# Attention and feed-forward on one core: the main loop in two 64-row tiles of the array, q and k work in fixed bursts

## The chip, the cores and the metric

The kernel runs on one core of one Trainium2 chip. A core has TensorE (PE in the profile; its weight loads are listed apart as PEld), VectorE (DVE), ScalarE (ACT), GpSimd (POOL) and SyncE (SP), which here only issues DMAs. The metric is the device time of one execution in microseconds (us).

## The reference

```
for each of 4 batches (N = 12480 rows, C = 128, 49 agents):
    a2k = softmax(scale * agents @ k.T)        # 49 x N
    agent_v = a2k @ v                          # 49 x 128
    q2a = softmax(scale * q @ agents.T)        # N x 49
    x = q2a @ agent_v                          # N x 128
h = x @ w_in                                   # 49920 x 2048
out = (h - tanh(h)) @ w_out                    # 49920 x 128
```

The softmaxes subtract the row maximum and divide by the sum plus 1e-9. All inputs are float32; w_in and w_out arrive as float64.

## The kernel before

Agent_v is never multiplied with q2a on its own: `project` forms agent_v @ w_in (49 x 2048) for each batch, and the first product of the loop is q2a with that. To keep float32 accuracy with the single-pass fp32r matmul, every operand is split into a high part, rounded to fp32r, and a low part, the rest.

**The loop.** Columns of the transposed problem are worked in 100 blocks of up to 500 (25 for each batch), and each block in 8 steps (`HP`), one for two of the 16 chunks of 128 hidden features: 800 steps in `fast`. Two blocks make a pair, 16 positions (`pos`). A step holds:

- `m1` (L534, L535): h, two PSUM banks of 128x500. The 98 rows are 49 of the high part of q2a and 49 of its low part (pT); the weights awh and awl hold the 49 rows of the projection twice. Four matmuls.
- `act`: ACT makes y = tanh (L544) and z = y squared (L546) for 1000 columns; DVE multiplies g = h * z (L549). (For the small h of these inputs h - tanh(h) is so approximated; a general path exists behind a run-time test and is not taken.)
- `high`: POOL rounds g to gh (L578). `low`, one step later: DVE makes gl = g - gh (L583).
- `m2`, a step later again: six matmuls of 128 rows into one accumulator (L596 gh with the low part of w_out, L597 gh with the high part, L598 gl with the high part). The first block and one step of every second block use one float32 product instead (L594), without gh and gl.
- `finish`: ACT copies the accumulator out (L754), and one store is issued for two blocks.

**Beside it.** For each pair of blocks `q_softmax` works on q: scores on PE (L490), row maximum on DVE (L498), copy out of PSUM on ACT (L499), subtraction on POOL (L501), exp, sum and division, rounding and low part (L511, L513); `q_transpose` makes pT (L521, L526). For the next batch `phase1` makes the k scores (L278, with their copy and maximum), later exp, transposes (L329) and the product with v (L339), one group of eight 128-row tiles at a time.

**What sets the order.** The jobs are generators; a step advances every live job once between `m1` and `act`. A scheduler orders the instructions of each engine from that; only for the first block is the order on DVE and ACT, and up to there on PE, tied to the program (`issue_order`). PSUM's eight banks are three two-bank buffers for h and two single banks ("misc") for accumulators, q, k and transposes. Matmuls on all 128 rows and columns have one tile shape; the k bursts L278 and L339 use two column tiles of 64.

Of the kernel before, what the change touches and what calls it, by code (L numbers as in the profile page):

```python
# [12 lines left out]
F32 = mybir.dt.float32  # L13
# [11 lines left out]
A = 49  # L25
A2 = 2 * A
EARLY = 11
HALF = 64
FF = 2048
# [6 lines left out]
NG = -(-NT // GT)  # L36
TAIL = N - KT * 128
# [17 lines left out]
KV = 3  # L55
# [4 lines left out]
LAG2 = 1  # L60
NB = dict(y=2, z=2, g=4, gh=3, gl=2)
# [4 lines left out]
QS = 3  # L66
T0 = 13
T1 = 2
KS = (4, 10, 15)
VS = (5, 10, 13)  # L70
# [26 lines left out]
class Build:  # L97
    def __init__(self, ctx, tc, aps):
# [6 lines left out]
        self.ph = ctx.enter_context(self.pool("ph", 3, space=PSUM))  # L105
        self.pmisc = ctx.enter_context(self.pool("pmisc", 2, space=PSUM))
# [6 lines left out]

    def misc(self):
        return self.pmisc.tile([128, 512], F32, tag="misc", name="misc")

    def constants(self):
# [13 lines left out]
        self.ones = c.tile([128, 128], F32, tag="ones", name="ones")  # L131
        nc.vector.memset(self.ones, 1.0)
# [7 lines left out]
        self.avs = c.tile([128, B, A2], F32, tag="avs", name="avs")  # L140
# [54 lines left out]
    def phase1(self, b):  # L195
# [36 lines left out]
        def scores(g):  # L232
            yield
            yield
            if g == 0:
                st["s"] = self.keep.tile([128, NG * 512], F32, tag="s", name="s", bufs=1)
                if b == 0:
                    st["mxp"] = self.work.tile([128, A, 2 * NG], F32, tag="mxp", name="mxp", bufs=1)
                else:
                    st["mxp"] = self.small.tile([128, NG], F32, tag="mxk", name="mxk")  # L240
                st["acc"] = self.small.tile([128, C + 1], F32, tag="acc", name="acc")
            n = tiles(g)
            kt = ahead("k", load_k, g, 1 if b == 0 else kb - 1)
            if b and g >= NG - vb:
                ahead("v", load_v, 0, g - NG + vb + 1)
            if b == 0:
                ps = self.ph.tile([128, 2, 512], F32, tag="h", name="h")
# [24 lines left out]
                return  # L272
            ps = self.misc()
            w = n // 2 * 128
            for c in range(n // 2):
                for r in range(2):
                    to = ps[HALF * r : HALF * (r + 1), c * 128 : (c + 1) * 128]
                    nc.tensor.matmul(to, self.agz[:, b, :], kt[:, n // 2 * r + c, :], start=True, stop=True)  # L278
            yield
            nc.scalar.copy(st["s"][:, g * 512 : g * 512 + w], ps[:, :w])  # L280
            nc.vector.tensor_reduce(st["mxp"][:, g : g + 1], ps[:, :w], axis=AX.X, op=ALU.max)
# [34 lines left out]
        def av(g):  # L316
            vt = ahead("v", load_v, g, vb - 1) if b else None
            n = tiles(g)
            if b:
                w = n // 2 * 128  # L320
                e = st["s"][:, g * 512 : g * 512 + w]
                first = self.count()
                nc.scalar.activation(e, e, AF.Exp, bias=st["mb"], scale=SCALE)
                self.hold(first, self.act_at, (ET.Activation,))
                yield
                ps = self.misc()
                for c in range(n // 2):
                    sl = slice(c * 128, (c + 1) * 128)
                    nc.tensor.transpose(ps[:, sl], e[:, sl], self.ident)  # L329
                yield  # L330
                et = self.small.tile([128, 512], F32, tag="ke", name="ke")
                nc.scalar.copy(et[:, :w], ps[:, :w])
                yield
                ps = self.misc()
                for c in range(n // 2):
                    for r in range(2):
                        t = n // 2 * r + c
                        k = rows(g, t)
                        nc.tensor.matmul(  # L339
# [294 lines left out]
    def fast(self):  # L634
# [86 lines left out]
        for tag in ("y", "z", "g"):  # L721
            self.wtile(tag, NB[tag])
# [180 lines left out]
```

## Time and profile before

| | |
|---|---|
| median of 3 runs | 2153.54 us (2152.6 to 2153.64) |
| span of the profiled execution, first to last instruction | 2150.6 us |
| PE busy at a granted clock of | 0.998 of full speed |
| start of the first block's first matmul | 54.4 us |

The page gives the profiled execution its span and no time of its own; the median of the runs is 2.9 us above it. In the lines below a group is a line of the kernel, an engine, an operation, the tile written and the tiles read, the shapes, and the count; behind the first bar stand the busy time and the mean duration in ns, behind the second the idle time of the engine ahead of the group and what ended it. A line of the timeline has the start and the duration in us ahead of the same names. "Busy" of PE counts a matmul until its modelled end, so two that follow each other closely overlap.

### The profile page before, as it was taken

The page shows a single profiled execution, that of the slowest core. Times are in us where ns is not written, and L with a number is a line of the kernel's source. Part 1 is how long each engine was busy: PE and PEld are TensorE (multiplying, and loading weights), DVE is VectorE, ACT ScalarE, POOL GpSimd, SP SyncE. Part 2 cuts the span into 40 slices and gives each one's busy share as a digit, 9 for nine tenths or more (in the row PEclk, how much of TensorE's full clock was granted, in tenths as well). Part 3 has the DMA queues.
Part 4 walks back from the last instruction along what each step waited for, and adds up shares of the span by engine and source line. Part 5 has one row for each costly group of instructions (what it writes and reads, how often), then busy time and mean ns, then how long its engine had stood idle before and what let it go on. Part 6 is the DMA issues. An engine that isn't in the chain of part 4 may idle for free.

```text
span 2150.6 us, 30293 instructions
## 1 busy us (share of the span) xinstructions
PE 2126.8 (99%) x10859; PEld 1713.6 (80%) x10859; DVE 1998.3 (93%) x2031; ACT 1828.1 (85%) x2136; POOL 1313.8 (61%) x858
## 2 busy tenths in 40 slices
PE   8999999999999999999999999999999999999998
PEld 7587878877877887888787778878878888888886
DVE  7999998889999998889999999988999999999998
ACT  3888888888888888888898888888889889899896
POOL 0365566556665565556675557655566767777666
PEclk9999999999999999999999999999999999999999
DMA  9321112110111111111002110111000000000000
GB/s 350 96 67 60 52 34 73 51 49 29 39 49 59 60 50 49 59 61 49 20 20 68 59 42 28 51 59 41 28 31 20 29 30 20 29 29 20 29 10 21
DMA packets 65325, 108.69 MB, mean 51 GB/s; under 512 B 3984, under 2 KB 44176, under 8 KB 65168
## 3 DMA queue, kind: packets, MB, share of 16 engines
q1 hardware_dynamic: 65168, 106.68, 15.1%
q8 instruction: 89, 1.46, 0.3%
q14 instruction: 68, 0.56, 0.1%
HBM read 81.10 MB, written 25.56 MB: 50 GB/s over the span
## 4 chain that ended last, share of the span: by engine, by line
PE 95%; DVE 2%; POOL 1%; issue 1%; ACT 0%; DMA 0%; POOLq 0%; SPq 0%; DVEq 0%
PE h L534 17%; PE h L535 16%; PE misc L598 16%; PE misc L596 15%; PE misc L597 15%; PE misc L594 4%; PE misc L490 4%; PE misc L339 2%; PE misc L278 2%; PE misc L521 1%; PE h L249 1%; POOL gh L578 1%; DVE g L549 1%; PE misc L329 1%; DVE gl L583 1%
## 5 line engine op out<-in xcount | busy, mean ns | idle before, releaser
L578 POOL TENSOR_SCALAR gh<-g 128x1000 fp32r<-128x1000 f32 (+1 forms) x743 | 1172.7, 1579 | 702.9 <-DVE g L549 357.9
L583 DVE TENSOR_TENSOR gl<-g,gh 128x1000 fp32r<-128x1000 f32 (+1 forms) x743 | 952.8, 1284 | 99.9 <-PE misc L598 58.9
L549 DVE TENSOR_TENSOR g<-h,z 128x1000 f32<-128x1000 f32 (+1 forms) x800 | 946.1, 1187 | 24.6 <-ACT z L546 20.6
L544 ACT ACTIVATE y<-h 128x1000 f32<-128x1000 f32 (+1 forms) x800 | 799.0, 1002 | 191.6 <-PE h L535 187.6
L546 ACT ACTIVATE z<-y 128x1000 f32<-128x1000 f32 (+1 forms) x800 | 828.8, 1040 | 21.2 <-DVE g L549 4.2
L534 PE MATMUL h<-pT,awh 98*128 98x500 f32 (+1 forms) x1600 | 662.1, 414 | 0.1
L535 PE MATMUL h<-pT,awl 98*128 98x500 f32 (+1 forms) x1600 | 623.1, 389 | 0.0
L598 PE MATMUL misc<-gl,wo_h 128*128 128x500 f32 (+1 forms) x1486 | 589.5, 397 | 3.7 <-DVE gl L583 3.7
L596 PE MATMUL misc<-gh,wo_l 128*128 128x500 f32 (+1 forms) x1486 | 579.0, 390 | 2.8 <-POOL gh L578 2.8
L597 PE MATMUL misc<-gh,wo_h 128*128 128x500 f32 (+1 forms) x1486 | 578.1, 389 | 0.0
L534 PEld LDWEIGHTS h<-pT,awh 98*128 98x128 f32 x1600 | 301.2, 188 | 77.4 <-issue 14.0
L535 PEld LDWEIGHTS h<-pT,awl 98*128 98x128 f32 x1600 | 303.0, 189 | 67.7 <-issue 14.7
L598 PEld LDWEIGHTS misc<-gl,wo_h 128*128 128x128 f32 x1486 | 279.1, 188 | 70.0 <-DVE gl L583 10.5
L596 PEld LDWEIGHTS misc<-gh,wo_l 128*128 128x128 f32 x1486 | 280.8, 189 | 62.6 <-POOL gh L578 7.8
L597 PEld LDWEIGHTS misc<-gh,wo_h 128*128 128x128 f32 x1486 | 279.7, 188 | 54.5
L501 POOL TENSOR_TENSOR qe<-qe,qm 126x392 f32<-126x392 f32 x50 | 69.7, 1395 | 65.3 <-ACT qe L499 65.3
L513 POOL TENSOR_TENSOR pp<-qe,pp 126x392 fp32r<-126x392 f32 x50 | 67.8, 1357 | 58.4 <-ACT pp L511 56.6
L490 PEld LDWEIGHTS misc<-ag,qt 128*126 128x126 f32 x800 | 95.9, 190 | 3.9
L490 PE MATMUL misc<-ag,qt 128*126 128x49 f32 x800 | 93.4, 269 | 0.0
L594 PE MATMUL misc<-g,wo_f 128*128 128x500 f32 (+1 forms) x196 | 89.9, 581 | 0.0
L754 ACT ACTIVATE o<-misc 128x500 f32<-128x500 f32 (+1 forms) x100 | 58.2, 582 | 21.7 <-PE misc L598 11.7
L526 ACT CAST pT<-misc 98x500 fp32r<-98x500 f32 (+1 forms) x100 | 56.7, 568 | 7.4 <-PE misc L521 6.5
(111 smaller groups left out, 840.5 us busy)
## 6 DMA issues: line engine op xcount, KB each, us to landing
kt<-kT SPq DMA_DIRECT2D x48, 512.0 KB, 3.7
qt<-qT SPq DMA_DIRECT2D x46, 500.0 KB, 3.4
outT<-o SPq DMA_DIRECT2D x46, 500.0 KB, 2.6
v<-v SPq DMA_DIRECT2D x36, 512.0 KB, 4.1
vt<-v SPq DMA_DIRECT2D x12, 512.0 KB, 7.1
raw<-w_in SPq DMA_DIRECT2D x4, 512.0 KB, 9.0
v<-w_out SPq DMA_DIRECT2D x4, 512.0 KB, 8.9
qt<-qT SPq DMA_DIRECT2D x4, 490.0 KB, 3.4
```

Source lines behind the costliest of these rows:

```text
L490: nc.tensor.matmul(ps[:TT, t * A : (t + 1) * A], qt[:, at : at + TT], self.ag[:, b, :], start=True, stop=True)
L534: nc.tensor.matmul(h[:, c, :w], aw[0][:A2, sl], pT[:A2, :w], start=True, stop=False)
L535: nc.tensor.matmul(h[:, c, :w], aw[1][:A2, sl], pT[:A2, :w], start=False, stop=True)
L544: nc.scalar.activation(self.pair(y), h, AF.Tanh, scale=TSC)
L546: nc.scalar.activation(z, y, AF.Square)
L549: nc.vector.tensor_tensor(self.pair(g), h, self.pair(z), ALU.mult)
L578: self.nc.gpsimd.tensor_scalar(gh, g, 1.0, 0.0, ALU.mult, ALU.add)
L583: self.nc.vector.tensor_tensor(gl, g, gh.bitcast(F32), ALU.subtract)
L594: nc.tensor.matmul(acc[:, :w], wf[:, c * C : (c + 1) * C], gh[:, x], start=first, stop=last)
L596: nc.tensor.matmul(acc[:, :w], self.wo_l[:, f, :], gh[:, x], start=first, stop=False)
L597: nc.tensor.matmul(acc[:, :w], self.wo_h[:, f, :], gh[:, x], start=False, stop=False)
L598: nc.tensor.matmul(acc[:, :w], self.wo_h[:, f, :], gl[:, x], start=False, stop=last)
```

## The change

- **First product.** `m1` has three terms for each chunk, all of 49 rows: awh with the low part, awl with the high part, awh with the high part. The matmuls of the first chunk use rows 0 to 48, those of the second rows 64 to 112, each with its own PSUM bank, in turn. For this pT holds the high part in rows 0 to 48 and the low part in rows 64 to 112, and two DMAs make pb, the same with the halves swapped. awh and awl hold their 49 rows at 0 and at 64.
- **Second product.** `m2` cuts each matmul into rows 0 to 63 and 64 to 127 with an accumulator each (two banks). ACT copies both (1000 columns), POOL adds them, and each block has its own store. It follows four steps behind `m1`, not two.
- **PSUM** is one pool of four two-bank buffers for everything; within one step all jobs may share a buffer.
- **q and k work.** k is worked two groups at a time, in 7 score and 7 product jobs for a batch; a job starts at positions 4 and 9, q at position 2, the transposes at 2 and 12. Jobs start inside the step, ahead of `act`. At the end the order of PE, DVE and ACT is tied to the program for the whole loop.
- The square is made in place (no z); gh has 4 buffers, gl and y 3.

```diff
-LAG2 = 1
-NB = dict(y=2, z=2, g=4, gh=3, gl=2)
+LAG2 = 3
+NB = dict(y=3, g=4, gh=4, gl=3)
...
-KS = (4, 10, 15)
-VS = (5, 10, 13)
+T0 = 12
+KS = (4, 9)
...
-        self.ph = ctx.enter_context(self.pool("ph", 3, space=PSUM))
-        self.pmisc = ctx.enter_context(self.pool("pmisc", 2, space=PSUM))
+        self.ph = ctx.enter_context(self.pool("ph", 4, space=PSUM))
+        self.share(False)
...
     def misc(self):
-        return self.pmisc.tile([128, 512], F32, tag="misc", name="misc")
+        if self.spare is not None:
+            ps, self.spare = self.spare, None
+            return ps
+        t = self.banks("misc")
+        if self.sharing:
+            self.spare = t[:, 1, :]
+        return t[:, 0, :]
...
         yield
-        pT = self.keep.tile([128, BLK], F32R, tag="pT", name="pT", bufs=3)
-        nc.scalar.copy(pT[:A2, :w], ps[:A2, :w])
-        res.append(pT)
+        pT = self.keep.tile([128, BLK], F32R, tag="pT", name="pT", bufs=2)
+        nc.scalar.copy(pT[:PW, :w], ps[:PW, :w])
+        pb = self.keep.tile([128, BLK], F32R, tag="pb", name="pb", bufs=2)
+        nc.sync.dma_start(pb[HALF:PW, :w].bitcast(F32), pT[:A, :w].bitcast(F32))
+        nc.sync.dma_start(pb[:A, :w].bitcast(F32), pT[HALF:PW, :w].bitcast(F32))
+        res.append((pT, pb))
...
-        for c in range(2):
-            sl = slice((2 * i + c) * 128, (2 * i + c + 1) * 128)
-            nc.tensor.matmul(h[:, c, :w], aw[0][:A2, sl], pT[:A2, :w], start=True, stop=False)
-            nc.tensor.matmul(h[:, c, :w], aw[1][:A2, sl], pT[:A2, :w], start=False, stop=True)
+        h = self.banks("h")
+        high, low = pT, pT[::-1]
+        for n, (weights, p) in enumerate(((aw[0], low), (aw[1], high), (aw[0], high))):
+            for c, r in enumerate((slice(0, A), slice(HALF, PW))):
+                sl = slice((2 * i + c) * 128, (2 * i + c + 1) * 128)
+                nc.tensor.matmul(h[:, c, :w], weights[r, sl], p[c][r, :w], start=n == 0, stop=n == 2)
...
+            terms = (low, gh), (high, gh), (high, gl)
+        for k, (weights, g) in enumerate(terms):
+            for c in range(2):
+                f = 2 * i + c
+                for r in range(2):
+                    rows = slice(HALF * r, HALF * (r + 1))
+                    nc.tensor.matmul(
+                        acc[:, r, :w],
+                        weights(f, c)[rows],
+                        g[rows, c * w : (c + 1) * w],
...
-            nc.scalar.activation(o[:, at : at + w], acc[n][:, :w], AF.Copy, scale=GSC)
...
+            nc.scalar.activation(o[:, :, :w], acc[n][:, :, :w], AF.Copy, scale=GSC)
+            nc.gpsimd.tensor_tensor(o[:, 0, :w], o[:, 0, :w], o[:, 1, :w], ALU.add)
+            nc.sync.dma_start(self.outT[:, column(n) : column(n) + w], o[:, 0, :w])
...
+            self.share(True)
+            if p + 1 < npair:
+                if pos == QL and p:
+                    qt[p + 1] = self.q_load(q_src(p + 1))
+                if pos == T0:
+                    live.append(t_job(2 * p + 2))
+                if pos == T1 and p:
+                    q = q_job(p + 1)
+                    next(q)
+                    live.append(q)
+            if pos == T1 and p:
+                live.append(t_job(2 * p + 1))
+            if pos in KS and kq and n:
+                live.append(kq.pop(0))
...
         finish(done.pop(0))
+        self.issue_order(ET.PE, early)
+        self.issue_order(ET.DVE, at)
+        self.issue_order(ET.Activation, at)
```

In the changed kernel the lines are L576 for the first product, L638 for the second, L585 and L586 for tanh and square, L588 for g, L617 for gh, L622 for gl, L525 for the q scores, L533, L534 and L536 for their maximum, copy and subtraction, L558 and L563 for the transposes and pT, L792 and L793 for the copy and the add at the end of a block. Names carry buffer numbers here; a row in brackets names the engines whose semaphores it waits for.

DVE before, around the maximum of a q job in the third batch (g_11333 belongs to one step, g_11366 to the next):

```order
L549 TENSOR_TENSOR g_11333<-h_11319,z_11331 128x1000 [waits Activation_49]
L498 TENSOR_REDUCE qm_11324<-misc_11289 126x8 [waits PE_49]
L583 TENSOR_TENSOR gl_11337<-g_11307,gh_11309 128x1000 [waits PE_49,Pool_49]
L549 TENSOR_TENSOR g_11366<-h_11345,z_11364 128x1000 [waits Activation_49]
L583 TENSOR_TENSOR gl_11370<-g_11333,gh_11335 128x1000 [waits PE_49,Pool_49]
```

DVE of the changed kernel, the same job (g_14127 belongs to position 2, g_14165 to position 3):

```order
L588 TENSOR_TENSOR g_14127<-h_14104,y_14124 128x1000 [waits PE_49,Activation_49]
L622 TENSOR_TENSOR gl_14131<-g_14086,gh_14088 128x1000 [waits PE_49,Pool_49]
L533 TENSOR_REDUCE qm_14152<-misc_14111 126x8
L588 TENSOR_TENSOR g_14165<-h_14145,y_14162 128x1000 [waits PE_49,Activation_49]
L622 TENSOR_TENSOR gl_14169<-g_14127,gh_14129 128x1000 [waits PE_49,Pool_49]
```

The maximum stood between a g and a gl and now stands directly ahead of a g.

ACT before, at the copy of the same job's scores:

```order
L544 ACTIVATE y_11362<-h_11345 128x1000 [waits PE_49]
L546 ACTIVATE z_11364<-y_11362 128x1000 [waits DVE_49,Activation_49]
L499 COPY qe_11325<-misc_11289 126x392 [waits DVE_49]
L544 ACTIVATE y_11386<-h_11378 128x1000 [waits PE_49]
L546 ACTIVATE z_11388<-y_11386 128x1000 [waits Activation_49]
L503 ACTIVATE qe_11325<-qe_11325 126x392 [waits Pool_49]
```

ACT of the changed kernel, at the same place:

```order
L586 ACTIVATE y_14124<-y_14124 128x1000 [waits Activation_49]
L534 COPY qe_14153<-misc_14111 126x392 [waits DVE_49,PE_49]
L563 CAST pT_14157<-misc_14111 113x500 [waits DMAHW5_49,DMAHW4_49]
L585 ACTIVATE y_14162<-h_14145 128x1000 [waits PE_49]
L586 ACTIVATE y_14162<-y_14162 128x1000 [waits Activation_49]
L792 ACTIVATE o_14190<-acc_13944 128x1000 [waits DMAHW7_49,PE_49,Pool_49]
```

The copy waits for DVE's maximum in both. Before, the tanh and square for the g behind the maximum (y_11362, z_11364) stand ahead of the copy; in the changed kernel (y_14162) they stand behind it and behind the copy of pT.

PE of the changed kernel at the same position: first product, q burst with transposes, second product.

```order
L576 MATMUL h_14104<-pb_13966,awh_11386 128x500 [waits DVE_49]
L576 MATMUL h_14104<-pT_13964,awh_11386 128x500
L576 MATMUL h_14104<-pT_13964,awl_11387 128x500
L576 MATMUL h_14104<-pb_13966,awl_11387 128x500
L525 MATMUL misc_14111<-ag_67,qt_14053 126x49 [waits DVE_49]
L558 MATMUL misc_14111<-identr_75,pp0_95 113x126 x4
L638 MATMUL acc_13944<-gh_14002,wo_l_86 128x500 [waits Pool_49]
L638 MATMUL acc_13944<-gh_14002,wo_h_85 128x500 x4
```

The q scores now stand between the two products of one step and wait for a g of DVE, since their PSUM buffer is one that h uses too.

270 lines of the change are left out of this document (132 added, 138 removed).

## The prediction

> **What bounds the kernel now.** I read the busy shares and the chain of work first, then the busy times by stretch, then the groups of instructions, then the timeline where one duration had to be understood.
>
> ```profile
> span 2150.6 us, 30293 instructions
> PE 2126.8 (99%) x10859; PEld 1713.6 (80%) x10859; DVE 1998.3 (93%) x2031; ACT 1828.1 (85%) x2136; POOL 1313.8 (61%) x858
> PE 95%; DVE 2%; POOL 1%; issue 1%; ACT 0%; DMA 0%; POOLq 0%; SPq 0%; DVEq 0%
> core 0: us, PE busy (x) PEld busy (x) DVE busy (x) ACT busy (x) POOL busy (x), PEclk, DMA share, GB/s
> 130.00:2120.00 1990.00, 1987.07 (x10004) 1604.68 (x10003) 1865.43 (x1846) 1727.18 (x1990) 1262.53 (x814) 1.00 0.13 41
> 1669.40:2100.20 430.80, 430.80 (x2004) 352.43 (x2003) 415.17 (x396) 383.58 (x429) 303.14 (x188) 1.00 0.07 25
> 657.00:1631.00 974.00, 972.55 (x5010) 782.10 (x5007) 903.78 (x907) 838.79 (x978) 594.06 (x390) 1.00 0.14 45
> ```
>
> The reader is to see two things. PE is busy 1987 of the 1990 us of the loop and makes 95% of the chain: it sets the pace. But DVE is close behind it, 1865 of 1990. In the last batch (1669 to 2100), where no k work runs, it is at 96%; in the middle stretch, with k work, at 93%. So whatever is taken off PE, DVE's idle time in the loop, 1990 - 1865.4 = **124.6 us**, is the most that can come out before DVE is the bound. A later loss on DVE counts in full.
>
> **PE, part by part.** One pair of chunks (a "step", 800 in all) costs PE four matmuls for the first product and six for the second.
>
> ```profile
> L534 PE MATMUL h<-pT,awh 98*128 98x500 f32 (+1 forms) x1600 | 662.1, 414 | 0.1
> L535 PE MATMUL h<-pT,awl 98*128 98x500 f32 (+1 forms) x1600 | 623.1, 389 | 0.0
> 1000.75 0.38 PE L534 MATMUL h<-pT,awh 98*128 98x500 f32 x1
> 1000.97 0.39 PE L535 MATMUL h<-pT,awl 98*128 98x500 f32 x1
> 1001.20 0.39 PE L534 MATMUL h<-pT,awh 98*128 98x500 f32 x1
> 1001.20 0.19 PEld L535 LDWEIGHTS h<-pT,awl 98*128 98x128 f32 x1
> ```
>
> From start to start a 500-column matmul takes 0.227 us (1000.97 - 1000.75 is 0.22, the next 0.23); the 0.39 is latency. The first product becomes six matmuls of 49 rows in three pairs, one of each pair in rows 0 to 48 and one in rows 64 to 112. If a pair costs what one full matmul costs, a step saves one 0.227 us: 800 x 0.227 = 182 us of PE. The second product has twelve matmuls of 64 rows in six pairs, so it stays at six slots. The trace of before has no pair of row tiles; the nearest are its column tiles.
>
> ```profile
> L278 PE MATMUL misc<-kt,ag 128*64 128x128 f32 x588 | 41.6, 280 | 0.0
> 227.97 0.39 PE L535 MATMUL h<-pT,awl 98*128 98x500 f32 x1
> 228.29 1.09 PE L278 MATMUL misc<-kt,ag 128*64 128x128 f32 x16
> 229.32 0.50 PE L598 MATMUL misc<-gl,wo_h 128*128 128x500 f32 x1
> 229.65 0.39 PE L596 MATMUL misc<-gh,wo_l 128*128 128x500 f32 x1
> ```
>
> Sixteen of them, 0.28 us each, are through in 1.09 us: two halves of the array work at once, loads too. I take the pair at one slot; the bounds are one slot and two. The same rows price a change of tile shape: L535 to L278 takes 0.32 instead of 0.23, L598 to L596 0.33 instead of 0.23, and something is lost at the burst's own end; I take 0.3 us for going out of a shape and back. Before, only the k bursts leave the common shape, 81 times in the loop by the order of the program; after, every q, transpose, k and projection burst does, 168 times: 87 x 0.3 = 26 us more. PE so falls by some 156 us, to about 1831 of the old 1990. It is no longer the bound, and the time does not follow it.
>
> **DVE.** Its work per step is untouched: one L549 (now L588) and one L583 (now L622). What is moved is the q softmax. In the changed order DVE runs the row maximum of the q scores (L533), and directly behind it the product g of that step (L588). ACT stands q's copy out of PSUM (L534) and a copy of pT (L563) ahead of that step's tanh and square, and the copy waits for DVE's maximum. So g waits for a chain that starts with the instruction before it: maximum, copy, copy, tanh, square, g. Nothing else stands between on DVE. In the order of before the tanh and square of the next g stand ahead of the copy, and a gl (L583) follows the maximum, so the chain is covered.
>
> ```profile
> L499 ACT COPY qe<-misc 126x392 f32<-126x392 f32 x50 | 23.9, 479 | 25.4 <-DVE qm L498 25.4
> L526 ACT CAST pT<-misc 98x500 fp32r<-98x500 f32 (+1 forms) x100 | 56.7, 568 | 7.4 <-PE misc L521 6.5
> L544 ACT ACTIVATE y<-h 128x1000 f32<-128x1000 f32 (+1 forms) x800 | 799.0, 1002 | 191.6 <-PE h L535 187.6
> L546 ACT ACTIVATE z<-y 128x1000 f32<-128x1000 f32 (+1 forms) x800 | 828.8, 1040 | 21.2 <-DVE g L549 4.2
> ```
>
> The first row shows that the wait for the maximum is real in before too (25.4 us). The gap is 0.48 + 0.57 + 1.00 + 1.04 = 3.09 us, less a tenth where ACT's instructions overlap: 3.0 us for each of 48 q jobs in the loop, **144 us** of idle DVE (bounds: 0 if DVE had to idle there anyway, 149 without the overlap).
>
> **The new add on POOL.** ACT now copies both accumulators (1000 columns instead of 500), and POOL adds them, 128x500 from two inputs, 100 times. Before has four such instructions in the loop, L190.
>
> ```profile
> L190 POOL TENSOR_TENSOR wo_l<-awh,wo_h x4: 1278/1290/1293, 81.3 to 96.7; 128x512 fp32r<-128x512 f32 x4
> L583 DVE TENSOR_TENSOR gl<-g,gh x743: 1141/1191/2272, 84.2 to 2142.1; 128x1000 fp32r<-128x1000 f32 x179, 128x960 fp32r<-128x960 f32 x7
> 93.43 1.29 POOL L190 TENSOR_TENSOR wo_l<-awh,wo_h 128x512 fp32r<-128x512 f32 x1
> 93.59 2.18 DVE L583 TENSOR_TENSOR gl<-g,gh 128x1000 fp32r<-128x1000 f32 x1
> 1707.47 1.19 DVE L583 TENSOR_TENSOR gl<-g,gh 128x1000 fp32r<-128x1000 f32 x1
> 1708.57 1.19 DVE L549 TENSOR_TENSOR g<-h,z 128x1000 f32<-128x1000 f32 x1
> 1709.68 1.19 DVE L583 TENSOR_TENSOR gl<-g,gh 128x1000 fp32r<-128x1000 f32 x1
> L578 POOL TENSOR_SCALAR gh<-g 128x1000 fp32r<-128x1000 f32 (+1 forms) x743 | 1172.7, 1579 | 702.9 <-DVE g L549 357.9
> ```
>
> A gl that meets L190 takes 2.18 us instead of 1.19: it stands still for 1.0 us. Bounds for an add: nothing, where it falls beside a g, and 1.0. I take three of four adds to be met: 100 x 0.78 = **78 us**, near the upper end because a DVE without idle time leaves few openings: g and gl alternate every 1.11 us, and POOL's own gh needs the openings already. All gl together lose 743 x (mean 1.284 - median 1.191) = 69 us in before, mostly around gh and the two q operations of POOL. One of those now falls into the 3.0 us gap, where no gl runs: I take off 20 us of the 69 (bounds 0 and 35).
>
> The Trainium skill, page "SBUF — State Buffer", section "Who interferes with whom", says that a VectorE instruction with two SBUF inputs and a GpSimd one that reads SBUF exclude each other for a whole instruction. The 2.18 us row agrees; by the rule at its worst every add costs its whole 1.29 us, 129 us instead of 78, and the time would be some 51 us longer.
>
> **Edits at nothing.** The square in place and the deeper rings (gh 4, gl 3, second product four steps behind the first instead of two) leave the instructions as they are. The two transfers per block that build the swapped copy pb are 98 KB:
>
> ```profile
> ag<-agT SPq DMA_DIRECT2D x1, 98.0 KB, 2.3
> kt<-kT SPq DMA_DIRECT2D x48, 512.0 KB, 3.7
> ```
>
> They are issued one step after the transposes, three steps (8 us) or more before the block starts, and land in about 2.3 us; SP's queue ahead of them holds k, v, q loads and the stores, which wait for work of the same or an earlier step. If that cover is gone, each block start loses up to 1 us, 100 us. The k loads now come two together, five steps (13 us) before their use, against 3.7 us; their burst of two groups replaces two bursts. ACT's doubled copy, 100 x 0.42 = 42 us (L544's 1.00 less L754's 0.58), lies in ACT's idle time of 263 us in the loop; at the end it and the add make the tail 1.7 us longer.
>
> ```profile
> L754 ACT ACTIVATE o<-misc 128x500 f32<-128x500 f32 (+1 forms) x100 | 58.2, 582 | 21.7 <-PE misc L598 11.7
> ```
>
> **The sum**, on the profiled 2150.6 us: - 124.6 (DVE's idle time, freed with PE) + 144 (gap) + 78 (adds) - 20 (q operation in the gap) + 2 (tail) = 2230.0. The median of the runs is 2153.54, 2.9 above the span; I add it: **2233 us**, 3.7% slower.
>
> **Rivals.**
> *The saving comes through (ends faster).* DVE and POOL alternate without meeting, at the pace of 1706 to 1712, where every gl takes 1.19: then the adds cost nothing and the old 69 us go too. 2150.6 - 124.6 + 144 - 69 + 2 + 2.9 = 2106. It decides below 48 us of such waits in all (2150.6 - 124.6 + 144 + 2 = 2172 without the 69, against 2150.6: the waits must fall by 21 from 69, adds included). For it: that stretch exists. Against it: 100 more POOL instructions. Chance 0.22; no change, where the waits come out just there, 0.06.
> *More stalls.* The four two-bank PSUM buffers hold h, accumulator and bursts. In the step of a burst h has two buffers, the burst waits for a g of two steps before, and the second product is queued behind it. With 0.5 to 1 us of idle DVE for each of 168 bursts: +84 to +168, 2317 to 2401. Before has the same shortage only in part, so I give it 0.12.
> *Row tiles take turns.* If two 49-row halves did not work at once, a step would hold 18 slots instead of 10: 2150.6 + 800 x 8 x 0.227 + 2.9 = 3606 us. PE becomes the bound over DVE once a pair costs about 0.26 us instead of 0.227 ((2230 - 1995) / 7200 pairs = 0.033; 1995 is 2150.6 less PE's 156). For it: no row of before shows two row tiles at work. Against: the column tiles. Chance 0.06.
> The Trainium skill, page "TensorE: Matmul & The Clock Gate", section "LDWEIGHTS (loading the stationary operand)", says that a load's time follows its columns and not its rows, which speaks against cutting by rows: 18 loads of 128 columns per step instead of 10. The 98- and 128-row loads of before both take 0.19, so the trace agrees; one after the other they would hold 18 x 0.19 = 3.4 us of a step, and PE would take some 900 us more.
>
> **How the numbers follow.** Forecast 0.54 for 2165 to 2310 us, the rivals as given. The range, 2105 to 2310, takes in the price of an add from 0 to 1.3 and the waits of gl from none to more than now; it leaves out most of the last two rivals and a little below. About 0.2% is what a measurement of this kernel can tell from no change. Faster 0.22, within 0.2% 0.06, slower 0.72 (0.54 + 0.12 + 0.06).
>
> **What would show it.** Right: DVE is the largest share of the chain, PE's busy share falls below 97%, g (L588) idles about 140 us on ACT's square, once per pair of blocks, ACT's q copy waits for the maximum, and the mean gl rises above 1.30 us beside the add. Wrong: PE still fills the loop (a pair costs more than one slot), the idle before g is small, or gl's mean falls to 1.19.

## The result, and the profile after

| | before | changed |
|---|---|---|
| median of the runs, us | 2153.59 (4 runs, 2152.6 to 2154.4) | 2374.47 (4 runs, 2372.66 to 2375.54) |
| ratio | 1 | 1.1022, 95% interval 1.1007 to 1.1038 |
| span of the profiled execution, us | 2150.6 | 2373.5 |

10.2% slower, where 3.7% was forecast and 2310 us was the upper end of the range. The page of the changed kernel, then its waits and the busy times of its loop:

```profile
PE 2108.6 (89%) x17145; PEld 1692.9 (71%) x17145; DVE 2023.3 (85%) x2003; ACT 1863.6 (79%) x2082; POOL 1553.5 (65%) x961
PE 35%; DVE 33%; ACT 16%; issue 13%; DMA 2%; POOL 0%; SPq 0%; DVEq 0%; ACTq 0%; POOLq 0%
L588 DVE TENSOR_TENSOR g<-h,y 128x1000 f32<-128x1000 f32 (+1 forms) x800 | 953.2, 1192 | 292.6 <-ACT y L586 284.2
L622 DVE TENSOR_TENSOR gl<-g,gh 128x1000 fp32r<-128x1000 f32 (+1 forms) x743 | 963.9, 1297 | 16.9 <-PE acc L638 14.9
L793 POOL TENSOR_TENSOR o<-o 128x500 f32<-128x500 f32 (+1 forms) x100 | 126.0, 1260 | 92.1 <-ACT o L792 92.1
L534 ACT COPY qe<-misc 126x392 f32<-126x392 f32 x50 | 24.4, 487 | 194.2 <-DVE qm L533 145.4
```

```profile
DVE g L588 <- ACT y L586: 284.2, 211, 3.1
PEld h L576 <- DVE g L588: 132.9, 136, 2.5
PE h L576 <- DMA pb<-pT: 7.3, 9, 1.1
```

```profile
130.00:2340.00 2210.00, 1972.31 (x16055) 1584.55 (x16053) 1894.76 (x1827) 1766.12 (x1943) 1494.65 (x911) 0.97 0.15 46
```

(A wait: total us, times, longest us. A window: its length, then busy time and count of PE, PEld, DVE, ACT and POOL, the granted clock of PE, and DMA.) No engine is full any more: the chain is shared by PE, DVE and ACT. DVE idles 2210 - 1894.8 = 315 us in the loop, against 124.6 before; its busy time grew by 29. The 220 us of the loop are thus 191 us more idle and 29 more busy. 284 of DVE's 350 us of idle in the whole span (2373.5 - 2023.3) stand ahead of g and are ended by ACT's square.

A second reading gives the place. The table has the mean time in us from the start of one g to the next, by the position of the first of the two, over the ten pairs of blocks from step 624 to 783 (last batch, no k work). A plain step is 2.22: one g and one gl. The last column is the sum over 16 positions.

| kernel | 2 | 3 | 4 | 10 | 11 | 12 | 13 | pair |
|---|---|---|---|---|---|---|---|---|
| before (its jobs stand elsewhere) | | | | | | | | 39.18 |
| changed | 5.86 | 2.86 | 2.56 | 2.22 | 2.35 | 4.64 | 2.54 | 44.65 |
| q_copy_first | 3.70 | 2.86 | 2.56 | 2.22 | 2.35 | 3.45 | 2.22 | 40.99 |
| t0_at_10 | 5.84 | 2.86 | 2.55 | 3.97 | 2.99 | 2.49 | 2.22 | 44.54 |
| t0_10_m1_thrice | 6.64 | 2.86 | 2.55 | 2.45 | 2.86 | 2.56 | 2.22 | 43.77 |
| cf_m2_full | 4.60 | 2.44 | 2.43 | 2.22 | 2.34 | 2.83 | 2.43 | 41.77 |
| cf_defer | 4.02 | 2.28 | 3.12 | 2.22 | 2.35 | 3.05 | 2.50 | 41.20 |
| cf_defer_gl4 | 2.69 | 3.96 | 2.22 | 2.22 | 2.34 | 3.05 | 4.41 | 42.51 |

In this batch the changed kernel loses at position 2, where the q burst and its softmax begin, and at position 12, where the next transposes and the new accumulator meet. Its plain steps are at DVE's floor. A "burst" here is a run of short matmuls for q, k or the transposes that PE works between the two products of a step.

### The profile page after: what moved, and what is told of

It is laid out like the page before. It is cut to its first block, busy times and chain, and to the rows that moved or that the text cites. A ratio compares the mean times of both kernels' runs of the same rounds, so it can differ in the third digit from the quotient of the medians.

```text
span 2373.5 us, 43563 instructions
## 1 busy us (share of the span) xinstructions
PE 2108.6 (89%) x17145; PEld 1692.9 (71%) x17145; DVE 2023.3 (85%) x2003; ACT 1863.6 (79%) x2082; POOL 1553.5 (65%) x961
## 4 chain that ended last, share of the span: by engine, by line
PE 35%; DVE 33%; ACT 16%; issue 13%; DMA 2%; POOL 0%; SPq 0%; DVEq 0%; ACTq 0%; POOLq 0%
PE acc L638 20%; DVE gl L622 14%; DVE g L588 14%; PE h L576 9%; ACT y L585 7%; ACT y L586 5%; PE misc L525 2%; ACT o L792 1%; ACT pT L563 1%; DVE qm L533 1%; DMA kt<-kT 1%; PE ks L311 1%; DVE qs L540 1%; DVE qs L541 1%; PE misc L342 1%
## 5 line engine op out<-in xcount | busy, mean ns | idle before, releaser
L617 POOL TENSOR_SCALAR gh<-g 128x1000 fp32r<-128x1000 f32 (+1 forms) x743 | 1333.0, 1794 | 549.6 <-DVE g L588 472.4
L588 DVE TENSOR_TENSOR g<-h,y 128x1000 f32<-128x1000 f32 (+1 forms) x800 | 953.2, 1192 | 292.6 <-ACT y L586 284.2
L622 DVE TENSOR_TENSOR gl<-g,gh 128x1000 fp32r<-128x1000 f32 (+1 forms) x743 | 963.9, 1297 | 16.9 <-PE acc L638 14.9
L585 ACT ACTIVATE y<-h 128x1000 f32<-128x1000 f32 (+1 forms) x800 | 799.0, 999 | 85.5 <-PE h L576 85.0
L586 ACT ACTIVATE y<-y 128x1000 f32<-128x1000 f32 (+1 forms) x800 | 831.6, 1039 | 25.4
L576 PE MATMUL h<-pb,awh 49*128 49x500 f32 (+1 forms) x1600 | 671.5, 420 | 115.2 <-DVE g L588 78.5
L576 PE MATMUL h<-pT,awh 49*128 49x500 f32 (+1 forms) x1600 | 672.6, 420 | 0.0
L638 PE MATMUL acc<-gh,wo_l 64*128 64x500 f32 (+1 forms) x2972 | 502.0, 410 | 70.0 <-DVE g L588 45.6
L638 PE MATMUL acc<-gh,wo_h 64*128 64x500 f32 (+1 forms) x2972 | 479.3, 394 | 0.0
L638 PE MATMUL acc<-gl,wo_h 64*128 64x500 f32 (+1 forms) x2972 | 476.7, 392 | 0.3
L576 PEld LDWEIGHTS h<-pb,awh 49*128 49x128 f32 x1600 | 302.8, 189 | 217.4 <-DVE g L588 132.9
L638 PEld LDWEIGHTS acc<-gh,wo_l 64*128 64x128 f32 x2972 | 291.3, 192 | 139.2 <-POOL gh L617 66.9
L638 PEld LDWEIGHTS acc<-gh,wo_h 64*128 64x128 f32 x2972 | 308.0, 190 | 40.7
L638 PEld LDWEIGHTS acc<-gl,wo_h 64*128 64x128 f32 x2972 | 304.6, 190 | 44.4 <-DVE gl L622 4.3
L576 PEld LDWEIGHTS h<-pT,awh 49*128 49x128 f32 x1600 | 303.4, 190 | 25.5 <-issue 3.8
L576 PE MATMUL h<-pb,awl 49*128 49x500 f32 (+1 forms) x800 | 313.4, 392 | 0.0
L576 PE MATMUL h<-pT,awl 49*128 49x500 f32 (+1 forms) x800 | 313.1, 391 | 0.0
L793 POOL TENSOR_TENSOR o<-o 128x500 f32<-128x500 f32 (+1 forms) x100 | 126.0, 1260 | 92.1 <-ACT o L792 92.1
L534 ACT COPY qe<-misc 126x392 f32<-126x392 f32 x50 | 24.4, 487 | 194.2 <-DVE qm L533 145.4
L576 PEld LDWEIGHTS h<-pT,awl 49*128 49x128 f32 x800 | 154.4, 193 | 18.0 <-issue 8.8
L576 PEld LDWEIGHTS h<-pb,awl 49*128 49x128 f32 x800 | 154.2, 193 | 9.2 <-issue 4.2
```

The costliest lines, as they stand in the source:

```text
L534: nc.scalar.copy(ev, pv)
L576: nc.tensor.matmul(h[:, c, :w], weights[r, sl], p[c][r, :w], start=n == 0, stop=n == 2)
L585: nc.scalar.activation(self.pair(y), h, AF.Tanh, scale=TSC)
L586: nc.scalar.activation(y, y, AF.Square)
L588: nc.vector.tensor_tensor(self.pair(g), h, self.pair(y), ALU.mult)
L617: self.nc.gpsimd.tensor_scalar(gh, g, 1.0, 0.0, ALU.mult, ALU.add)
```

## The experiments

Times are medians; the kernel before took 2153.4 to 2154.7 us beside them, and the ratios are to it. "cf" names kernels that start from q_copy_first.

**q_copy_first: the wait for the maximum taken away.**

```diff
-        nc.vector.tensor_reduce(m[:TT], pv, axis=AX.X, op=ALU.max)
         nc.scalar.copy(ev, pv)
+        nc.vector.tensor_reduce(m[:TT], ev, axis=AX.X, op=ALU.max)
```

> ACT copies the q scores out of PSUM without waiting for DVE, and DVE takes the row maximum from that copy; everything else stays. Theory A (the chain maximum, copy, pT copy, tanh, square, g is what DVE idles for at position 2: 147 us between L533 and L588 in the changed kernel): the chain now starts when the square of position 2 ends, about 2.2 + 0.5 us earlier, so 2.6 of the 3.06 us of each of 48 gaps go: about -125 us, 2250 us, and the idle time of g behind the maximum falls below 40 us. Rival (the burst on PE, q scores and transposes of 2.3 us ahead of the second product, is late in any case, and the tanh waits for PE instead): above 2340 us, and the idle time of g stays, now ended by PE's h.

2249.0 us, 1.0443 (1.0425 to 1.046): 125.5 us less. The groups of DVE in it:

```profile
L588 DVE TENSOR_TENSOR g<-h,y 128x1000 f32<-128x1000 f32 (+1 forms) x800 | 953.1, 1192 | 178.0 <-ACT y L586 173.2
L534 DVE TENSOR_REDUCE qm<-qe 126x8 f32<-126x392 f32 x50 | 27.7, 554 | 1.2 <-ACT qe L533 1.2
```

111 of g's 284 us of idle are gone, and position 2 fell by 2.16 us, some 104 us over 48 pairs. Between the maximum and the next g DVE idled 147 us in the changed kernel and idles 44 here, so 103 us of the gap are shown to be this wait (the 44 miss the expected 40). The other 22 us of the gain lie elsewhere: in the last batch at positions 12 and 13, 1.5 us a pair, where the changed kernel runs at half clock and this one does not. The last section says why that need not come from the edit.

**no_add: the add on POOL left out.** 

> Leaves out POOL's add of the two accumulators (L793); the first half alone is stored, so the output is not the sum. ACT's copy of 1000 columns stays. By the prediction's price the adds cost 78 us: 2297 us. By the mean of gl in the profile (1297 ns against 1284 before, 743 times) they cost about 10 us: 2360 to 2375 us.

2365.4 us, 1.0981 (1.0963 to 1.0999): 9 us less. The same two groups:

```profile
L588 DVE TENSOR_TENSOR g<-h,y 128x1000 f32<-128x1000 f32 (+1 forms) x800 | 953.9, 1193 | 327.9 <-ACT y L586 320.6
L622 DVE TENSOR_TENSOR gl<-g,gh 128x1000 fp32r<-128x1000 f32 (+1 forms) x743 | 914.2, 1230 | 14.4 <-PE acc L638 12.4
```

With the add the mean gl is 1297 ns, so the adds do block gl for 743 x 0.067 = 50 us; but g idles 36 us longer without them. They fall into time in which DVE waits anyway. The expected 2297 us, by the prediction's price, did not come; 2360 to 2375 did.

**order_first_block and before_order: the fixed order.** The first ties the order only for the first block, as before; the second ties the kernel before for the whole loop.

> The order of PE, DVE and ACT is tied to the program for the first block only, as in the kernel before; the rest of the change stays. Theory D (the fixed order is what puts q's copy and the burst ahead of the work that DVE needs next): the scheduler moves them out of the way and the 147 us behind the maximum and some of the stall at position 12 go: 2130 to 2250 us. Rival (jobs started ahead of tanh, and four shared PSUM buffers, cost the time in any order): above 2340 us.

> The kernel before, with the order of PE, DVE and ACT tied to the program for the whole loop, that one part of the change alone. If the fixed order itself costs time: 2200 us and more, with the maximum's gap in it. If it costs only together with the jobs' place ahead of tanh and with the four buffers: 2140 to 2175 us. In the changed kernel freeing the order cost 146 us.

2519.8 us (1.169) and 2927.4 us (1.3599). Theory D falls: freed, the order costs the changed kernel 145 us more, which is in the rival's range. In the kernel before the fixed order does cost time by itself, 773 us, where the second expectation had 2200 us and more. So the price of the order depends on the rest of the kernel. That the second product four steps behind is what makes the fixed order bearable is a guess; no run tried it alone.

**t0_at_10 and t0_10_m1_thrice: where the transposes stand, and PE's clock.** `T0 = 10` instead of 12; the second also makes the first product of that position three times.

> The transposes for the next pair start at position 10 instead of 12; everything else stays. In the changed kernel g to g takes 4.64 us on average at position 12 in the last batch, 2.42 more than a plain step. Theory B (position 12 is where the second product opens a new accumulator: old accumulator, two h, transposes and new accumulator are five users of four PSUM buffers, so PE stands for a g of the step before, 1.7 us, and the next h is late): away from there the burst fits, at least half of 48 x 2.4 = 116 us goes: 2260 to 2320 us. Rival (a burst of transposes costs this wherever it stands): 2365 to 2385 us, with the long step at position 10 instead.

> The transposes at position 10 (2374 us), and the first product of that position made three times over, with the same result: 2 x 6 matmuls of 0.23 us per pair in three rows of pairs, 1.4 us more work for PE in each of 50 pairs, in the place of most of the 1.36 us in which PE waits for the burst's buffer. Theory F (after that idle time PE is granted half its clock for 3.4 us, and the second product behind it takes 2.67 instead of 1.35 us): with PE kept busy the clock stays, and the time falls although PE does more: 2310 to 2360 us, mean clock up from 0.964. Rival (the clock does not matter, or h comes later by the repeats): 2374 to 2445 us.

2374.3 us (1.1023, 1.1005 to 1.1041): no change, the long step moved along to 10 and 11. The meeting with the accumulator is not its cause. With the repeats 2384.4 us (1.1059), in the rival's range. In the last batch position 10 falls from 3.97 to 2.45, but position 2 grows by 0.8, and in the batches with k work nothing is gained. Position 10 without and with the repeats:

```profile
2174.63:2178.61 3.98, 3.98 (x26) 2.65 (x24) 2.30 (x4) 2.24 (x4) 2.80 (x2) 0.86 0.16 49
```

```profile
2195.99:2198.43 2.44, 2.44 (x18) 1.49 (x16) 2.30 (x4) 2.25 (x4) 2.06 (x2) 1.00 0.14 43
```

More work for PE made this step shorter, at full clock. As a remedy it fails. The changed kernel shows the clock on its own at position 12, PE's timeline (start, duration):

```profile
2180.64 0.72 PE L638 MATMUL acc<-gh,wo_l 64*128 64x500 f32 x4 [1.70 <-DVE g L588]
2182.52 0.62 PE L576 MATMUL h<-pb,awh 49*128 49x500 f32 x1
2182.94 0.62 PE L576 MATMUL h<-pT,awl 49*128 49x500 f32 x1
2185.68 0.38 PE L576 MATMUL h<-pb,awh 49*128 49x500 f32 x1
2185.71 0.39 PE L576 MATMUL h<-pT,awh 49*128 49x500 f32 x1
2185.90 0.38 PE L576 MATMUL h<-pT,awl 49*128 49x500 f32 x1
```

The second product waits 1.70 us for a g, since its new accumulator needs that g's h buffer. Then the matmuls take 0.62 instead of 0.38 us for some 3.4 us. The same position in the changed kernel and in q_copy_first:

```profile
2181.66:2186.17 4.51, 4.51 (x30) 4.21 (x28) 3.08 (x2) 2.47 (x3) 4.00 (x3) 0.63 0.22 77
```

```profile
2058.21:2061.66 3.45, 3.45 (x34) 3.06 (x32) 3.13 (x3) 2.52 (x4) 3.45 (x3) 1.00 0.14 53
```

At full clock the step is still 1.2 us over a plain one; another 1.1 goes with the half clock, in two kernels whose code differs only in the q job that starts at position 2.

**burst_after_m2, copy_first_burst_after: the order of burst and second product.** The block that starts and advances the jobs moves behind `out(LAG2)`, with T1, T0 and KS one less.

> The bursts of q, transposes and k on PE stand behind the second product of a step instead of ahead of it (started one position earlier, so that on ACT and DVE the jobs keep their places). Theory E (the wait of a burst for its PSUM buffer holds up the second product behind it, and then the next h): 1.35 us of second product are done during the wait. The gap behind the maximum stays (147 us). 48 x 2 bursts of q and transposes gain up to 1.35 us each, the k bursts some: 2240 to 2330 us. Rival (what counts is that the next first product stands behind both, in either order, or that DVE's gaps are all ACT's): 2360 to 2380 us.

> Both edits: ACT's copy of the q scores ahead of DVE's maximum, and the bursts behind the second product. If the two losses are separate (theories A and E), the gains add: 2249 less the gain of the bursts alone, 2110 to 2200 us, and the kernel may pass the one before (2154). If they are one wait seen twice: about 2249 us.

2453.8 us (1.1391) and 2306.3 us (1.0711): 79 and 57 us worse than without the move. Theory E's gain is not there, and none of the ranges was met. (Position 1 became long, 3.88 us; what the earlier start does to it was not separated.)

**half_second: PSUM cut as before.** 

> Leaves out the row tiles 64 to 127 of the second product, so the output is not the product; its slots on PE stay, since the two tiles of a pair run at once. The accumulator then takes one bank and PSUM is cut as in the kernel before: three two-bank buffers for h and two single banks for the accumulator and the small bursts (q scores and the transposes of position 2 still share a buffer of h; so do the k scores). ACT still copies 1000 columns (the one accumulator twice) and POOL still adds. Theory E (a burst or a second accumulator takes one of three h buffers; PE waits for a g of two steps before, the second product and the next h are late): with no such wait left at positions 8 to 15, g to g at position 12 falls from 4.64 to under 3.0 us in the last batch, and the whole to 2230 to 2290 us. Rival (pT's copy ahead of the tanh, or the transposes on PE, make the long step): position 12 stays above 4 us and the whole above 2340 us.

3283.4 us (1.5235): neither. PE was granted 0.58 of its clock and set the pace, so the run tells nothing of PSUM; see the last section.

**cf_m2_full: the second product as before.**

```diff
-                for r in range(2):
-                    rows = slice(HALF * r, HALF * (r + 1))
...
+                nc.tensor.matmul(
+                    acc[:, :w],
+                    weights(f, c),
+                    g[:, c * w : (c + 1) * w],
...
```

> ACT's copy ahead of DVE's maximum (2249 us), and the second product as in the kernel before: 128 rows, one accumulator of one bank, no add, 500 columns to copy; PSUM cut as before into three two-bank buffers for h and two single banks (q scores and the transposes of position 2 share a buffer of h, as do the k scores). The output is the reference's. The first product stays in row tiles, so PE changes shape twice in each of 800 steps. By 0.3 us for going out of a shape and back a step holds 3 + 6 slots of 0.227 and 0.3, 2.35 us, and PE sets the pace again: 2190 to 2225 us, PE busy over 97%. Theory E (PSUM buffers) expects the long step at position 12 to go with it, whatever the pace: no more than 0.8 us over the median step of the last batch. Rival for the first number: the changes of shape cost nothing, then DVE's 2.22 us stay and the time falls to 2140 to 2180. Rival for the second: pT's copy on ACT makes the long step, position 12 stays 1.2 us over the others.

2311.5 us (1.0725), PE busy 98%, so PE sets the pace; a plain step takes 2.42 us. Back to back, without a change of shape, nine slots take 2.05 (q_copy_first, 2032.45 to 2034.50 on PE, below), so two changes cost 0.37 us a step, not 0.3. That is 56 us more over 800 steps; the time is 87 us above the expected range. Position 12 is 0.4 over the plain step, with pT's copy where it was: theory E's second number holds, though a slower pace hides more.

**cf_spread, cf_spread_warm, cf_spread_split: other places.** `T0 = 10`, `KS = (5, 13)`; then with the repeats; then with the q scores split over two steps.

> Copy ahead of the maximum (2249 us), and the bursts spread: transposes at position 10 instead of 12, k jobs at 5 and 13 instead of 4 and 9, so that no burst stands in the step that opens an accumulator (4 and 12) or next to another. If the meeting of bursts with the accumulator's switch or with each other costs time in the three batches with k work (44.23 us a pair of blocks here against 40.99 in the last batch): 2190 to 2235 us. If each burst costs its stall wherever it stands: 2240 to 2260 us.

> The same spread, and the first product of position 10 made three times over with the same result (1.4 us more PE work ahead of the transposes, 50 times), now away from k's bursts. Theory F (PE's half clock after waiting at the burst): in the last batch position 10 fell by 1.5 us with the repeats when it was tried on the changed kernel, and position 9 and 10 of the other batches, where a k burst stood, did not. Now all batches gain: 30 to 70 us below the kernel without the repeats. Rival: within 10 us of it, or above.

> The same spread, and the q job begins at position 1 with half of its scores, the other half follows at position 2 (with the maximum and the copies at position 3 as before, pT's copy at 2); the transposes stand at position 1. If the length of the q burst (2.5 us of PE between the two products) makes the steps at 2 and 3 long (3.70 and 2.86 us in the last batch, against 2.22 and 0.56 for the maximum): each falls towards 2.3, 40 to 90 us below the kernel without the split. Rival (the buffer, now held for one step more, costs as much): within 20 us, or above.

2259.6 us (1.0482, 1.0465 to 1.05), 2279.6 us (1.0566) and 2304.0 us (1.0699), all above 2249.0. The rivals' ranges hold: no other place for the bursts was cheaper.

**before_psum4: the four shared buffers alone.** 

> The kernel before, with its eight PSUM banks as four two-bank buffers for everything, as in the change; accumulators, q, k and transposes use one bank of a buffer each. Theory E (PSUM buffers): where PE sets the pace, two buffers left for h at a burst stop PE: 2190 to 2300 us, PE's busy share from 99% to under 97%. Rival (the cut of PSUM costs nothing, the stalls of the changed kernel come from the in-order bursts alone): 2150 to 2170 us.

2357.6 us, 1.0946 (1.0928 to 1.0964): this cut of PSUM alone costs the kernel before 203 us, more than either theory gave it. PE falls from 99% to 95%. The cut is tighter than the change's: here every small tile takes a whole two-bank buffer, while in the change the small tiles of one step may share one. So the 203 us are not a term of the changed kernel's time.

**cf_tiny_burst, cf_tiny_shared: a buffer taken for nothing.**

> Copy ahead of the maximum (2249 us), and at position 14 of each pair, a plain step of 2.2 us in all batches, a burst with next to no work is added: one transpose of 8 columns, and on ACT one copy of a single column a step later. It takes one of the four PSUM buffers from the wait for a g of two steps before until that copy. Theory E (taking a buffer is what a burst costs, whatever its work): the steps at 14 and 15 grow by 0.8 to 1.5 us together, +40 to +75 us. Rival (a burst costs its PE and ACT work): +5 to +20 us.

> The control for it: the same tiny transpose and copy, in the buffer of the transposes at position 12, so that no further buffer is taken and no further change of shape made. Both theories expect little; it tells the price of the two instructions alone: 0 to +20 us on 2249.

2273.8 us (1.0542) and 2266.6 us (1.0519, 1.0493 to 1.0546): 7 us apart. The first is 25 us above q_copy_first, between the two ranges. But positions 14 and 15 grew by only 0.08 us together (batches with k work), 0.15 in the last; there position 12, which the edit does not touch, grew from 3.45 to 4.71, at half clock. Theory E in its plain form falls: here a wait of one step for a buffer cost next to nothing, with little work behind it.

**cf_defer, cf_defer_gl4: the next first product ahead of the second.**

```diff
...
+            burst = n > 0 and any(j.engine == ET.PE for j in list(nc.cur_bb.bb.instructions)[first:])
...
-            out(LAG2)
+            out(LAG2 + burst)
```

> Copy ahead of the maximum (2249 us), and in a step with a burst on PE the second product is put off to the next step: burst, next first product, then two second products, instead of burst, second product, first product. Rings and PSUM stay. Theory E2 (after a burst's wait and its own 0.6 to 2.5 us, the 1.35 us of second product that stand ahead of the next first product are what makes the next h late: from the end of the g that frees the buffer to the next g PE and ACT need 2.5 + 1.45 + 0.7 + 2.05 = 6.7 us at position 2, DVE has work for 5.5 + 0.56): the excess of position 2 (0.9 us beside the maximum) and of position 12 (1.2 us) goes, in the three batches with k work more: 2130 to 2190 us. Rival (the buffers alone: h waits for the same g in either order): 2235 to 2260 us. A second rival (two second products in a row make the step after late, and gl waits for its ring): above 2260.

> The deferred second product again (2299 us), with four buffers for gl instead of three (room for it from one buffer of the output tile and from y and g of 1000 columns instead of 1024). In cf_defer DVE idled 114 us ahead of g on ACT's square instead of 173, but 91 us ahead of gl on the second product instead of 11. If these 80 us are gl's ring, full because the second product that frees it is put off: 2200 to 2235 us, below copy-first alone (2249), and theory E2 stands (the second product ahead of the next first product is what makes h late). If gh's ring or the clock takes its place, or E2 is wrong: 2250 to 2300 us.

2299.5 us (1.0668) and 2286.2 us (1.0613, 1.0599 to 1.0628). In the first gl waits for its ring, that is for one of its three buffers to come free:

```profile
L622 DVE TENSOR_TENSOR gl<-g,gh 128x1000 fp32r<-128x1000 f32 (+1 forms) x743 | 981.3, 1321 | 99.5 <-PE acc L638 90.8 <-POOL o L793 4.6 <-POOL gh L617 0.9
```

In the second that wait is gone, and position 2 falls to 2.69, the plain step and the maximum, as E2 wants; but position 3 rises to 3.96 and position 13 to 4.41. The work that was put off is late one step on. Three stretches of q_copy_first help to see why: positions 2 and 3, just behind the q burst, positions 10 and 11, and the plain positions 14 and 15:

```profile
2031.79:2038.31 6.52, 6.51 (x58) 5.16 (x56) 5.07 (x6) 5.19 (x7) 5.06 (x4) 1.00 0.33 106
2053.64:2058.21 4.57, 2.31 (x21) 1.69 (x19) 4.52 (x6) 4.51 (x6) 3.82 (x3) 1.00 0.00 0
2063.88:2068.32 4.44, 4.44 (x42) 3.77 (x40) 4.44 (x6) 4.38 (x5) 3.65 (x3) 1.00 0.01 5
```

and PE's timeline there:

```profile
2028.70 1.96 PE L525 MATMUL misc<-ag,qt 128*126 128x49 f32 x16
2030.48 0.59 PE L558 MATMUL misc<-identr,pp 126*113 126x126 f32 x4
2031.00 0.72 PE L638 MATMUL acc<-gh,wo_l 64*128 64x500 f32 x4
2032.45 0.39 PE L576 MATMUL h<-pb,awh 49*128 49x500 f32 x1
2034.50 0.39 PE L576 MATMUL h<-pT,awh 49*128 49x500 f32 x1
```

PE's busy share alone does not tell its limit: in the plain steps PE and DVE both count as full, though PE's nine slots need 2.05 of the 2.22 us. The rest tells more. At positions 10 and 11 DVE is full (4.52 of 4.57) and PE stands for half the time, waiting for a g to free a PSUM buffer (0.57 us ahead of the transposes, 1.70 ahead of the new accumulator). At the q burst one matmul follows the other on PE from 2028.70 to 2034.50, and at positions 2 and 3 DVE idles 1.45 us. PE cannot work ahead, because the buffers hold it to DVE, and after a burst it gains only 2.22 - 2.05 = 0.17 us a step. No version beat the kernel before; the best is q_copy_first.

## Why the prediction was wrong in size

By its own steps, the sum on the loop:

| term | forecast, us | measured, us |
|---|---|---|
| DVE's idle time, freed with PE | -124.6 | +44 (idle +191, less the gap's 147) |
| gap behind the maximum | +144 | +147 idle between L533 and g, 48 times; 103 of it gone in q_copy_first |
| adds, less the q operation in the gap | +58 | +29 more busy time; the adds are worth 9 us of time |

- **PE's slots**: right. Two row tiles work at once: in the changed kernel the two halves of a pair start at 2185.68 and 2185.71, and the next pair at 2185.90, 0.22 us later. The rival "row tiles take turns" did not come. The row from which the prediction read this did not show it: sixteen matmuls of 128 columns in 1.09 us is also about the pace of one after the other, 15 x 0.227 x 128 / 500 + 0.28 = 1.15 us. The single records of the trace do show it, in pairs that start 0.01 us apart, one pair every 0.11 us.
- **The gap**: right in place and cause, and in size as idle time (147 us for 144). Of the signs, the copy's wait for the maximum (145 us) and PE below 97% (89%) came. DVE does not lead the chain (PE 35%, DVE 33%), and gl's mean is 1.297, just under 1.30. That g idles about 140 us on the square, once per pair, came out as 284 us in 211 waits: this surplus is the step that failed.
- **The failed step** is "it is no longer the bound, and the time does not follow it", with the term "- 124.6 (DVE's idle time, freed with PE)". Totals over the loop were compared, DVE's against PE's. But the loop has stretches with different limits: DVE bounds the plain steps, PE the bursts, and neither makes up for the other. The term came out 168 us higher than forecast. It failed apart from the gap too: q_copy_first idles 2070.0 - 1870.9 = 199 us on DVE in its loop, 75 more than before, with 44 of them left behind the maximum:

```profile
130.00:2200.00 2070.00, 1917.95 (x15993) 1541.10 (x15995) 1870.90 (x1817) 1763.04 (x1936) 1482.29 (x907) 0.98 0.16 49
```

- The rival **"more stalls"** had this time (2317 to 2401) and part of the mechanism: four shared buffers, a burst that waits, a second product behind it. It was given 0.12. The sum put all this at nothing. The rival's price, the wait alone, is refuted at one place by cf_tiny_burst; what the stretches above point to is the burst's work behind the wait, paid in place, and at times PE's clock after it. before_psum4 shows that a still tighter cut costs 203 us where PE sets the pace. Before, there were five places, three for h alone, so "shortage only in part" made too little of it.
- **The adds**: their lock is there (50 us of gl, forecast 78), but it falls into idle time. The forecast took DVE to have none.
- **Covered edits**: right for pb, 7.3 us of waits in all.
- **Change of shape**: 0.37 us, not 0.3.

Of the 95 us by which q_copy_first is still slower than before, most does not need the half clock. Ten pairs of the last batch, before and in q_copy_first:

```profile
1713.01:2104.80 391.79, 391.79 (x1822) 320.38 (x1821) 378.16 (x362) 349.33 (x391) 276.45 (x171) 1.00 0.07 24
1781.32:2191.20 409.88, 374.02 (x3083) 299.00 (x3082) 386.10 (x361) 357.26 (x391) 312.43 (x191) 1.00 0.10 33
```

At a clock of 1.00 in both, q_copy_first takes 18.1 us longer: 10.2 us more idle time on DVE and 7.9 more busy. At that rate 48 pairs would lose 87 us (an estimate from these ten). What stays open is how much of this the four buffers make in the changed kernel, and how much the place of the bursts in a fixed order. A cut with three h buffers at full clock and unchanged shapes was not tried: both row tiles then write one bank, without an order between them.

## What to carry to other kernels

When an edit takes the bound engine below the next one, add up the larger of the two for each stretch, burst by burst; the sum of maxima is nearer the time than the maximum of sums, unless buffers let the faster engine run ahead. Count PSUM buffers by how many steps the product ahead may lead, and see what takes one of them away. A blocked instruction costs nothing on an engine that waits anyway, so price it only after the idle time is known. Read the granted clock of each stage before a difference of one per cent is put down to an edit.

## What the runs showed of the hardware

PE's clock was granted by more than whether PE is busy. In half_second, whose second product uses only rows 0 to 63, a late stretch of the loop reads:

```profile
3000.00:3066.00 66.00, 66.00 (x215) 50.89 (x212) 38.70 (x37) 36.47 (x39) 29.42 (x19) 0.50 0.06 20
```

PE is busy for all of 66 us at half clock; over the whole run the mean is 0.583, against 0.964 with both row tiles and 0.990 with full rows (cf_m2_full). The Trainium skill, page "TensorE: Matmul & The Clock Gate", section "What's actually happening", says that the gate follows how busy PE has been of late, in windows of about 3.4 us. The length agrees with position 12 above (about 3.4 us at half clock); here busy time alone does not, since 66 of 66 us did not lift the clock. How full the array is would fit; no run varied it alone.

The same page, section "HAM oscillation — how this bites in real kernels", gives idle gaps over about 3.4 us as the danger. In the changed kernel a gap of 1.70 us was followed by a half-speed stretch. In q_copy_first the same gap at position 12 was not:

```profile
2057.20 0.72 PE L638 MATMUL acc<-gh,wo_l 64*128 64x500 f32 x4 [1.70 <-DVE g L588]
2058.63 0.39 PE L576 MATMUL h<-pb,awh 49*128 49x500 f32 x1
```

Where the gap falls fits the difference. In the clock records of these two runs and of cf_tiny_burst every change of the clock lies on one grid of 3.41 us. Ahead of position 12 in the ten pairs of the last batch, PE stood for 1.65 to 2.26 us within one interval of that grid in the changed kernel, and half clock followed ten times. In q_copy_first the same waits lay across a line of the grid, at most 1.40 us in one interval, and half clock never followed; in cf_tiny_burst it was 1.48 to 1.82 us, and it followed ten times. The amount does not explain every case: 6 of the 43 intervals at half clock in the changed kernel's loop came after less than 1 us of standing. So whether a kernel pays for the half clock at position 12 can hang on how its pairs lie on the grid, and differences of 10 to 20 us between these kernels need not come from their edits.
